# Half chunks of the output's second channel half taken from eight PSUM banks, and what is reordered with them

## The chip, the cores and the metric

The kernel runs on one core of a Trainium2 chip. The metric is the device time of one execution in microseconds (us). Three executions of the kernel before the change took 295.18, 295.45 and 297.18 us; their median is 295.45 us.

## The reference

The input is q, k and v of shape 4 x 5056 x 256 and the weights of a soft mixture of experts (8 experts with 4 slots each, 32 slots in all). Cut to what matters:

```python
qn = q / (norm(q, axis=1) + 1e-6);  kn = k / (norm(k, axis=1) + 1e-6)
a = softmax(kn.transpose(0, 2, 1) @ qn / tau)          # 256 x 256 per batch
x = (v @ a).reshape(20224, 256)
logits = x @ phi                                       # 20224 x 32
slot_input = softmax_over_rows(logits).T @ x           # 32 x 256
slot_out[e] = relu(slot_input[e] @ w1[e]) @ w2[e]      # 4 slots per expert
c = softmax_over_slots(logits)                         # 20224 x 32
return c @ slot_out                                    # 20224 x 256, 20.7 MB
```

The last line is the part that the change touches: a product of 20224 x 32 by 32 x 256, whose result has to leave PSUM through two engines and the core through the DMA queues.

## The kernel before, in words

For some 210 us the core reads q, k and v, scores, normalizes, and reduces everything to the 32 slot inputs. Then comes the expert MLP (`up`, `flip_h`, `down`) and at last the output. The order on TensorE (PE), VectorE (DVE), ScalarE (ACT) and on SyncE's DMA queue (SP) is the order in which the code is written, so each engine takes its instructions as they stand and waits where an operand is not there.

The slot outputs (32 x 256) are made in two channel halves of 128. `down(0, ...)` makes the first half in PSUM tile `O`; `fetch(0)` copies it out on DVE (tile `ob`), and `spread(0)` multiplies it by a folding matrix (matmul `fo`, L902) and copies the result on ACT to `so_a` and `so`. With that the output's first half can start while `down(1, ...)` still makes the second half. The 16 steps of `down(1, ...)` are handed out by `more(MORE[u])` between the output pieces; each step is four matmuls in the code, eight in the trace, where each f32 product shows as two instructions. When all 16 are out, `fetch(1)` and `spread(1)` bring the second half to `so`.

The output rows come as 20 chunks of up to 1024 rows, in ten pairs (`PAIRS`). A pair has a tile `cT` of combine weights, turned by four transposes on PE (`flip_c`, tile `cTp`) and copied by ACT.

- The first four pairs (`HALVED = 4`) go out as half chunks of 512 KB: `half_chunk(i, z, h)` is pair i, chunk z, channel half h. The text calls the eight of the first channel half u0 to u7 and the eight of the second u8 to u15, in the order of the code. A half chunk is eight small matmuls into four PSUM tiles `oph` (L923; sixteen in the trace), four copies from PSUM to SBUF (`oh<-oph`, L926: tiles 0 and 2 by ACT, 1 and 3 by DVE) and one DMA (L927). The `oph` tiles come from pool `pq` with five banks.
- The other six pairs go out as whole chunks of 1 MB or 0.98 MB, o1 to o12 in the text: eight matmuls `op` of 256 columns (L991), four copies of 512 columns (L998), and DMAs (L1003), out of pool `po` with eight banks, which opens when the half chunks are done.

Ahead of each half chunk of the second channel half and of each whole chunk stands a product with the identity (L919, 256 columns; L988, 512 columns) into the first of its tiles, which the real matmuls then overwrite. The result doesn't depend on it.

Between the pieces DVE and ACT work on the softmax over slots of the later chunks: `combine_some(n)` takes the next n steps of a list (`top` L798, `less` L801, `total` L807 to L809, `share` L812 on DVE; `powers` L804 on ACT). `HALFC` and `POPS` say how many.

Of the kernel before, what the change touches and what calls it, by code (L numbers as in the profile page):

```python
# [8 lines left out]
F32 = mybir.dt.float32  # L9
# [8 lines left out]
def colnorm_attention_soft_moe(  # L18
# [11 lines left out]
    nc = tc.nc  # L30
    B, N, C = q.shape
    E, _, F = w1.shape
    P = 128
    J = 8
    S = 32
    G = 4
# [6 lines left out]
    HALVED = 4  # L43
    MLPC = (1, 2, 2, 2, 3, 2, 1, 1)
    FINAL = 1
    MORE = (0, 2, 2, 3, 3, 3, 3, 0)
    HALFC = (0, 1, 1, 1, 1, 0, 1, 0)
    POPS = (1, 0, 1, 0, 1, 0, 1, 0, 1, 1, 1, 1, 1, 1, 1, 1)
    LAG = 14
# [37 lines left out]
    ident = const.tile([P, P], F32, name="ident")  # L87
# [35 lines left out]
    def pieces(rows, ch, j0, j1):  # L123
        t0 = chunks[ch][0]
        jm = min(j1, JL) if ch == NCH - 1 else j1
        lo = t0 + P * j0
        yield slice(0, P), slice(j0, jm), rows[lo : lo + P * (jm - j0), :].rearrange("(p j) c -> p j c", j=jm - j0)
        if jm < j1:
            lo = t0 + P * JL
            yield slice(0, TL), slice(JL, J), rows[lo : lo + TL, :].rearrange("(p j) c -> p j c", j=1)  # L130
# [204 lines left out]
    def combine_some(n):  # L335
        while steps and (n or steps[0][0].__name__ == "powers"):
            f, h = steps.pop(0)
            f(h)
            stepped.append(f)
            n -= f.__name__ != "powers"  # L340
# [400 lines left out]
    def big(t, name):  # L741
        if t == "v":
            return vpool.tile([P, J, C], F32, tag="v", name=name)
        return wpool.tile([P, J, C], F32, tag=t, name=name, bufs=5)
# [18 lines left out]
    for step in TAIL.split():  # L763
# [13 lines left out]
        x = big("t", f"vt{pb_}_{ch}").rearrange("p (m x) c -> p m (x c)", m=2)  # L777
        n = min(P * J, N - chunks[ch][0])
# [83 lines left out]
    CH = C // 2  # L862
# [3 lines left out]
    def down(h, r, fs):  # L866
        for f in fs:
            for g in range(G):
                nc.tensor.matmul(  # L869
                    O[h][S * g : S * g + S, :],  # L870
                    hTs[r][:, f, S * g : S * g + S],
                    w2t[G * r + g][:, h, f * CH : f * CH + CH],
                    start=r == 0 and f == 0,
                    stop=r == 1 and f == NF - 1,
                )

    cTs = {}

    def flip_c(i, pool=None):
        tp = (pool or ps_t).tile([P, 4, P], F32, tag="op" if pool else "T", name=f"cTp{i}")  # L880
        for x in range(4):
            b, ch = divmod(PAIRS[i][x // 2], NCH)
            assert len(stepped) >= ready_at(b, ch), (i, len(stepped))
            t = ch * J + HJ * (x % 2)
            nc.tensor.transpose(tp[:, x, :], nat[b][:, t : t + HJ, :].rearrange("p j s -> p (j s)"), ident)  # L885
        cTs[i] = bpool.tile([P, J, P], F32, tag="vD", name=f"cT{i}", bufs=4)
        if pool:
            return tp
        nc.scalar.copy(cTs[i][:, :4], tp)

    so_a = bpool.tile([P, CH], F32, tag="aT", name="so_a")
    so = bpool.tile([P, C], F32, tag="ssb", name="so")
    obs, fos = [], []

    def fetch(h):
        ob = bpool.tile([P, C], F32, tag="gs" if h else "dg", name=f"ob{h}")[:, :CH]
        nc.vector.tensor_copy(ob, O[h])
        obs.append(ob)

    def spread(h):  # L900
        fo = ps_t.tile([P, 4, P], F32, tag="T", name=f"fo{h}")[:, 0]
        nc.tensor.matmul(fo, fold4, obs[h], start=True, stop=True)  # L902
        if h == 0:
            nc.scalar.copy(so_a, fo)
        nc.scalar.copy(so[:, CH * h : CH * h + CH], fo)

    halves = {}

    def half_chunk(i, z, h):
        if z == 0:  # L910
            halves[i, h] = vpool.tile([P, 2, J, CH], F32, tag="v", name=f"oh{i}_{h}")
        ot = halves[i, h][:, z]
        rhs = so[:, CH:] if h else so_a
        b, ch = divmod(PAIRS[i][0], NCH)
        r0 = b * N + chunks[ch][0] + P * J * h + P * HJ * z
        dst = out[r0 : r0 + P * HJ, :].rearrange("(p a) c -> p (a c)", p=P)
        ops = [pq.tile([P, 2, CH], F32, tag="op", name=f"oph{i}_{h}_{z}_{t}") for t in range(G)]
        if h:
            nc.tensor.matmul(ops[0].rearrange("p x c -> p (x c)"), ident, so, start=True, stop=True)  # L919
        for x in range(2):  # L920
            for t in range(G):
                rows = slice(S * t, S * t + S)
                nc.tensor.matmul(ops[t][:, x, :], cTs[i][rows, 2 * z + x, :], rhs[rows, :], start=True, stop=True)  # L923
        for t in range(G):
            copy = nc.vector.tensor_copy if t % 2 else nc.scalar.copy
            copy(ot[:, t::G, :], ops[t])  # L926
        nc.sync.dma_start(dst, ot.rearrange("p j c -> p (j c)"))  # L927
        if z and h:
            cTs.pop(i)
# [10 lines left out]
    pq = ps_h.enter_context(tc.tile_pool(name="pq", bufs=5, space=PSUM, reuse_waits="tile"))  # L940
# [12 lines left out]
    def more(n):  # L953
        for _ in range(n):
            r, f = second.pop(0)
            down(1, r, (f,))

    for u in range(2 * HALVED):
        more(MORE[u])
        if second == [] and len(obs) == 1:  # L960
            fetch(1)
        half_chunk(u // 2, u % 2, 0)
        if u in (2, 4):
            flip_c(u // 2 + 1)
        if u == 2 * HALVED - 2:
            spread(1)
        combine_some(HALFC[u])
    pops = iter(POPS)
    for i in range(HALVED):
        for z in range(2):  # L970
            half_chunk(i, z, 1)
            combine_some(next(pops, 0))
        if i == 1:
            flip_c(HALVED)
    ps_h.close()
    ps_m.close()
    ps_x.close()
    po = ctx.enter_context(tc.tile_pool(name="po", bufs=8, space=PSUM, reuse_waits="tile"))
    for i, pair in enumerate(PAIRS):
        if i < HALVED:  # L980
            continue
        cT = cTs.pop(i)
        for z, y in enumerate(pair):
            b, ch = divmod(y, NCH)
            ot = vpool.tile([P, J, C], F32, tag="v", name=f"o{b}_{ch}")
            ops = [po.tile([P, 2, C], F32, tag="op", name=f"op{b}_{ch}_{t}") for t in range(G)]
            held = cT[:, :4].rearrange("p x c -> p (x c)")
            nc.tensor.matmul(ops[0].rearrange("p x c -> p (x c)"), ident, held, start=True, stop=True)  # L988
            for x, t in [(x, t) for x in range(2) for t in range(G)]:
                rows = slice(S * t, S * t + S)  # L990
                nc.tensor.matmul(ops[t][:, x, :], cT[rows, 2 * z + x, :], so[rows, :], start=True, stop=True)  # L991
            n = min(next(pops, 0), len(steps))
            flip = z == 0 and i + 1 < len(PAIRS)
            if flip:
                tp = flip_c(i + 1, po)
            for t in range(G):
                copy = nc.scalar.copy if t % 2 == 0 or t == 1 and n and z else nc.vector.tensor_copy
                copy(ot[:, t::G, :], ops[t])  # L998
            if flip:
                nc.scalar.copy(cTs[i + 1][:, :4], tp)  # L1000
            combine_some(n)
            for ps, js, dst in pieces(out[b * N : b * N + N, :], ch, 0, J):
                nc.sync.dma_start(dst, ot[ps, js, :])  # L1003
# [52 lines left out]
```

## Time and profile before

| | |
|---|---|
| median of three executions | 295.45 us |
| the profiled execution's own time | 295.44 us |
| its span in the trace | 293.3 us |
| PE busy | 273.4 us, 93% |
| DVE busy | 226.9 us, 77% |
| ACT busy | 196.2 us, 67% |
| DMA | 113.03 MB, mean 385 GB/s |
| first output DMA issued | 234.06 us |
| last output DMAs issued | from 284.75 us |
| last matmul started, last DVE copy started | 282.9 us, 284.0 us |

The span runs from the first to the last instruction on the core; 2.14 us of the execution's time lie outside it. The 16 DMA engines are shared by all transfers, and "DMA share" is their mean busy share: 1.00 is full, and a window of two or three microseconds can show a little more. All times in the trace are counted from the span's start.

### The profile page before, as it was taken

The numbers are of one execution on the slowest core, as the hardware profiler recorded it, in microseconds if no ns is written. First come the engines' busy times: TensorE is split into PE (matmuls) and PEld (weight loads), VectorE is DVE, ScalarE is ACT, GpSimd is POOL, SyncE is SP. The second block draws the span as 40 slices with busy tenths as digits, with TensorE's granted clock in tenths as the row PEclk, the third lists the DMA queues.
The fourth block names the chain that finished last, engine by engine and source line by source line (L and its number), as shares of the span: only waits on it lengthen the run. The fifth ranks groups of instructions, "written<-read, shape, count | busy, mean of one in ns | idle before, by whom it ended". The sixth has DMA issues, their size and how long they took to land.

```text
span 293.3 us, 6456 instructions
## 1 busy us (share of the span) xinstructions
PE 273.4 (93%) x2552; PEld 211.7 (72%) x2552; DVE 226.9 (77%) x338; ACT 196.2 (67%) x321; POOL 8.4 (3%) x22
## 2 busy tenths in 40 slices
PE   7998999999999999999999999789999999999960
PEld 4787999788898788788878878466654776655520
DVE  1379997998898998989898992669777598768550
ACT  2698676797779799876989923545616474577540
POOL 0000001000010010001001001000000000000000
PEclk9999999999999999999999999999999999999995
DMA  6999999999999999899979999999999998979996
GB/s 218 417 416 405 398 404 421 415 426 370 408 404 422 422 370 381 345 407 358 393 306 327 401 419 401 421 425 405 421 417 416 394 362 328 374 312 404 400 423 257
DMA packets 27228, 113.03 MB, mean 385 GB/s; under 512 B 3264, under 2 KB 4288, under 8 KB 23104
## 3 DMA queue, kind: packets, MB, share of 16 engines
q1 hardware_dynamic: 27200, 112.64, 96.6%
q8 instruction: 20, 0.33, 0.4%
q14 instruction: 8, 0.07, 0.1%
HBM read 91.92 MB, written 20.71 MB: 384 GB/s over the span
## 4 chain that ended last, share of the span: by engine, by line
PE 58%; DVE 9%; ACT 6%; issue 4%; DVEq 0%; ACTq 0%
PE S L240 21%; PE L L388 4%; PE op L991 4%; PE G L516 4%; PE oph L923 4%; PE op L988 4%; PE O L869 3%; PE H L842 2%; DVE hl L203 2%; PE cTp L885 2%; PE oph L919 2%; PE vTp L361 2%; DVE all L219 2%; ACT et L464 1%; PE Mp L318 1%
## 5 line engine op out<-in xcount | busy, mean ns | idle before, releaser
L240 PE MATMUL S<-raw 128*128 128x256 f32 x364 | 84.9, 385 | 0.6 <-DMA raw<-in_k_dram 0.6
L209 ACT ACTIVATE sq<-raw 128x2048 f32<-128x2048 f32 x40 | 76.1, 1909 | 8.3 <-DMA raw<-in_k_dram 5.9
L240 PEld LDWEIGHTS S<-raw 128*128 128x128 f32 x364 | 68.0, 192 | 14.5 <-issue 5.9
L219 DVE TENSOR_TENSOR all<-all,sq 128x2048 f32<-128x2048 f32 x32 | 73.1, 2284 | 6.6 <-ACT sq L209 6.0
L240 PE MATMUL S<-hl 128*128 128x256 f32 x414 | 57.2, 290 | 2.8 <-DVE hl L203 2.6
L240 PEld LDWEIGHTS S<-hl 128*128 128x128 f32 x414 | 51.7, 191 | 5.6 <-DVE hl L203 4.0
L198 ACT CAST hl<-raw 128x1024 fp32r<-128x1024 f32 (+2 forms) x37 | 36.5, 987 | 15.6 <-PE S L240 14.6
L203 DVE TENSOR_TENSOR hl<-raw,hl 128x1024 fp32r<-128x1024 f32 (+2 forms) x37 | 42.5, 1147 | 5.4 <-ACT hl L198 5.4
L998 ACT COPY o<-op 128x512 f32<-128x512 f32 x27 | 14.4, 591 | 10.1 <-issue 4.8
L998 DVE COPY o<-op 128x512 f32<-128x512 f32 x21 | 13.7, 687 | 9.1 <-PE op L991 6.0
L516 PE MATMUL G<-v,dn 128*32 128x256 f32 x320 | 19.5, 381 | 1.3 <-ACT lt L404 1.1
L926 ACT COPY oh<-oph 128x256 f32<-128x256 f32 x32 | 10.3, 375 | 9.7 <-PE oph L923 8.6
L926 DVE COPY oh<-oph 128x256 f32<-128x256 f32 x32 | 12.0, 417 | 6.1 <-PE oph L923 6.0
L361 PE MATMUL vTp<-ident,v 128*128 128x128 f32 x120 | 16.1, 276 | 0.6 <-DVE ssb L291 0.6
L217 DVE TENSOR_TENSOR all<-sq,sq 128x2048 f32<-128x2048 f32 x4 | 9.1, 2268 | 9.7 <-ACT sq L209 9.7
L516 PEld LDWEIGHTS G<-v,dn 128*32 128x32 f32 x320 | 11.4, 110 | 6.2 <-ACT gs L532 1.7
L361 PEld LDWEIGHTS vTp<-ident,v 128*128 128x128 f32 x120 | 13.9, 146 | 2.2 <-DVE ssb L291 0.8
L991 PEld LDWEIGHTS op<-so,cT 32*128 32x128 f32 x192 | 8.7, 184 | 9.4 <-issue 9.1
L991 PE MATMUL op<-so,cT 32*128 32x256 f32 x192 | 13.8, 400 | 0.0
L373 ACT COPY vT<-vTp 128x512 f32<-128x512 f32 x22 | 11.8, 587 | 1.9 <-PE vTp L361 1.9
L988 PE MATMUL op<-cT,ident 128*128 128x512 f32 x24 | 13.0, 623 | 0.0
L388 PE MATMUL L<-vD,M 128*32 128x256 f32 (+1 forms) x144 | 11.5, 379 | 0.0
(130 smaller groups left out, 305.5 us busy)
## 6 DMA issues: line engine op xcount, KB each, us to landing
raw<-in_q_dram SPq DMA_DIRECT2D x35, 512.0 KB, 7.4
raw<-in_k_dram SPq DMA_DIRECT2D x35, 512.0 KB, 8.2
v<-in_v_dram SPq DMA_DIRECT2D x16, 1024.0 KB, 10.7
w<-in_moe_w_dram SPq DMA_DIRECT2D x8, 1024.0 KB, 13.8
w<-in_moe_w_dram SPq DMA_DIRECT2D x16, 512.0 KB, 10.0
out_dram<-oh SPq DMA_DIRECT2D x16, 512.0 KB, 3.7
out_dram<-o SPq DMA_DIRECT2D x8, 1024.0 KB, 6.2
vD<-in_v_rows_dram SPq DMA_DIRECT2D x15, 512.0 KB, 8.7
```

Source lines behind the costliest of these rows:

```text
L198: nc.scalar.copy(hl[u][:, 0, :, :ns], raw_of(u)[:, :, :ns])
L203: nc.vector.tensor_tensor(hl[u][:, 1, :, :ns], raw_of(u)[:, :, :ns], hl[u][:, 0, :, :ns].bitcast(F32), op=ALU.subtract)
L209: nc.scalar.activation(sq[u], raw_of(u), AF.Square)
L219: nc.vector.tensor_tensor(st[b]["all"], st[b]["all"], sq.pop(u), op=ALU.add)
L240: nc.tensor.matmul(sps[:, m, :], lhs, rhs, start=r == 0 and part == 0 and x == 0 and y == 0 and m == 0, stop=r == H - 1 and part == 1 and ...
L361: nc.tensor.transpose(tp[:, jj, :], vt[:, 4 * hh + jj, P * m : P * m + P], ident)
L388: nc.tensor.matmul(L[S * g : S * g + S, :je, :], M[:, m, :], st[b]["vT", ch, m][:, :je, S * g : S * g + S], start=m == 0, stop=m == 1,)
L516: nc.tensor.matmul(gp[S * g : S * g + S, :], tiles[c][:, j, :], vt[:, j, :], start=c == 0 and j < G, stop=c == n - 1 and j >= G,)
L926: copy(ot[:, t::G, :], ops[t])
L988: nc.tensor.matmul(ops[0].rearrange("p x c -> p (x c)"), ident, held, start=True, stop=True)
L991: nc.tensor.matmul(ops[t][:, x, :], cT[rows, 2 * z + x, :], so[rows, :], start=True, stop=True)
L998: copy(ot[:, t::G, :], ops[t])
```

## The change

It touches only what happens after 232 us.

- Pool `po` with its eight banks opens before the half chunks of the second channel half, and these take their tiles from it. For that, everything that uses the older pools has to be over: `fetch(1)` and `spread(1)` come right after u7, where `spread(1)` stood after u6. The transposes for the fifth pair (`flip_c(HALVED)`) also write a tile of `po`.
- `MORE` hands out the 16 steps of `down(1, ...)` in four visits of four (before u1, u3, u5, u7) instead of six visits of two or three (before u1 to u6).
- The turned combine weights of the third and fourth pair come after u1 and u3 instead of after u2 and u4.
- The identity product ahead of the half chunks stands only before every second one, as one of 256 and one of 128 columns; ahead of whole chunks it has 384 columns instead of 512.
- In u8, u10, u12 and u14, where DVE has a softmax step to do, ACT takes three of the four copies instead of two.

```diff
-    MORE = (0, 2, 2, 3, 3, 3, 3, 0)
+    MORE = (0, 4, 0, 4, 0, 4, 0, 4)
...
-    def half_chunk(i, z, h):
+    def half_chunk(i, z, h, n=0):
...
-        ops = [pq.tile([P, 2, CH], F32, tag="op", name=f"oph{i}_{h}_{z}_{t}") for t in range(G)]
-        if h:
-            nc.tensor.matmul(ops[0].rearrange("p x c -> p (x c)"), ident, so, start=True, stop=True)
+        ops = [banks[0].tile([P, 2, CH], F32, tag="op", name=f"oph{i}_{h}_{z}_{t}") for t in range(G)]
+        if h and not z:
+            for x in range(2):
+                nc.tensor.matmul(ops[x].rearrange("p x c -> p (x c)")[:, : C - x * CH], ident, so[:, : C - x * CH], start=True, stop=True)
...
-            copy = nc.vector.tensor_copy if t % 2 else nc.scalar.copy
+            copy = nc.scalar.copy if t % 2 == 0 or t == 1 and n else nc.vector.tensor_copy
...
+    banks = [pq]
     for u in range(2 * HALVED):
         more(MORE[u])
         if second == [] and len(obs) == 1:
             fetch(1)
         half_chunk(u // 2, u % 2, 0)
-        if u in (2, 4):
-            flip_c(u // 2 + 1)
-        if u == 2 * HALVED - 2:
-            spread(1)
+        if u in (1, 3):
+            flip_c(u // 2 + 2)
         combine_some(HALFC[u])
-    pops = iter(POPS)
-    for i in range(HALVED):
-        for z in range(2):
-            half_chunk(i, z, 1)
-            combine_some(next(pops, 0))
-        if i == 1:
-            flip_c(HALVED)
+    spread(1)
     ps_h.close()
     ps_m.close()
     ps_x.close()
     po = ctx.enter_context(tc.tile_pool(name="po", bufs=8, space=PSUM, reuse_waits="tile"))
+    banks[0] = po
+    pops = iter(POPS)
+    for i in range(HALVED):
+        for z in range(2):
+            n = next(pops, 0)
+            half_chunk(i, z, 1, n)
+            combine_some(n)
+        if i == 1:
+            tp = flip_c(HALVED, po)
+            nc.scalar.copy(cTs[HALVED][:, :4], tp)
...
-            nc.tensor.matmul(ops[0].rearrange("p x c -> p (x c)"), ident, held, start=True, stop=True)
+            nc.tensor.matmul(
+                ops[0].rearrange("p x c -> p (x c)")[:, : 3 * P], ident, held[:, : 3 * P], start=True, stop=True
+            )
```

Three places show how the order moves. In the names, `oph_0_1_3` is the PSUM tile of channel half 0, chunk 1 of its pair, tile 3, and the number behind it tells one tile from the next.

On PE between u5 and u6, before the change, steps of the second half of `O` stand between the two half chunks:

```order
L923 MATMUL oph_0_1_2_2629<-so_a,cT_2540 128x128
L923 MATMUL oph_0_1_3_2630<-so_a,cT_2540 128x128
L869 MATMUL O<-w_4_1845,hT_2384 32x128
L869 MATMUL O<-w_5_1847,hT_2384 32x128
L869 MATMUL O<-w_6_1849,hT_2384 32x128
```

At the same place of the change u6 follows u5 at once:

```order
L924 MATMUL oph_0_1_2_2625<-so_a,cT_2521 128x128
L924 MATMUL oph_0_1_3_2626<-so_a,cT_2521 128x128
L924 MATMUL oph_0_0_0_2641<-so_a,cT_2582 128x128
L924 MATMUL oph_0_0_1_2642<-so_a,cT_2582 128x128
L924 MATMUL oph_0_0_2_2643<-so_a,cT_2582 128x128
L924 MATMUL oph_0_0_3_2644<-so_a,cT_2582 128x128
```

So nothing on PE lies between the two any more, while the five banks of `pq` stay as they were.

On PE at the end of the first channel half, before: the spreading product `fo` stands between u6 and u7, and u7's eight matmuls come between it and the first use of `so` (the row with `ident`).

```order
L923 MATMUL oph_0_0_3_2662<-so_a,cT_2609 128x128
L902 MATMUL fo_2676<-ob_2656,fold_98 128x128
L923 MATMUL oph_0_1_0_2680<-so_a,cT_2609 128x128
L923 MATMUL oph_0_1_1_2681<-so_a,cT_2609 128x128
L923 MATMUL oph_0_1_2_2682<-so_a,cT_2609 128x128
L923 MATMUL oph_0_1_3_2683<-so_a,cT_2609 128x128
L923 MATMUL oph_0_1_0_2680<-so_a,cT_2609 128x128
L923 MATMUL oph_0_1_1_2681<-so_a,cT_2609 128x128
L923 MATMUL oph_0_1_2_2682<-so_a,cT_2609 128x128
L923 MATMUL oph_0_1_3_2683<-so_a,cT_2609 128x128
L919 MATMUL oph_1_0_0_2698<-so,ident 128x256
L923 MATMUL oph_1_0_0_2698<-so,cT_2452 128x128
```

The same place of the change, from u7's last two matmuls on:

```order
L924 MATMUL oph_0_1_2_2679<-so_a,cT_2582 128x128
L924 MATMUL oph_0_1_3_2680<-so_a,cT_2582 128x128
L902 MATMUL fo_2694<-ob_2675,fold_98 128x128
L920 MATMUL oph_1_0_0_2704<-so,ident 128x256
L920 MATMUL oph_1_0_1_2705<-so,ident 128x128
L924 MATMUL oph_1_0_0_2704<-so,cT_2452 128x128
```

`fo` moved behind u7, and the next matmul reads `so`, which ACT makes from `fo`'s result.

On DVE at the same place, before: the copy `ob` (L897) stands ahead of u6's copies (`oph_0_0`), and each half chunk has two copies.

```order
L897 COPY ob_2656<-O 128x128
L926 COPY oh_0_2658<-oph_0_0_1_2660 128x2x128
L926 COPY oh_0_2658<-oph_0_0_3_2662 128x2x128
L812 TENSOR_TENSOR nat_107<-nat_107,cm_0_1865 128x640
L926 COPY oh_0_2658<-oph_0_1_1_2681 128x2x128
L926 COPY oh_0_2658<-oph_0_1_3_2683 128x2x128
L926 COPY oh_1_2697<-oph_1_0_1_2699 128x2x128
L926 COPY oh_1_2697<-oph_1_0_3_2701 128x2x128
L807 TENSOR_REDUCE cm_1_1866<-nat_107 128x20
```

With the change:

```order
L927 COPY oh_0_2640<-oph_0_0_1_2642 128x2x128
L927 COPY oh_0_2640<-oph_0_0_3_2644 128x2x128
L812 TENSOR_TENSOR nat_107<-nat_107,cm_0_1865 128x640
L897 COPY ob_2675<-O 128x128
L927 COPY oh_0_2640<-oph_0_1_1_2678 128x2x128
L927 COPY oh_0_2640<-oph_0_1_3_2680 128x2x128
L927 COPY oh_1_2703<-oph_1_0_3_2707 128x2x128
L807 TENSOR_REDUCE cm_1_1866<-nat_107 128x20
```

`ob` moved behind u6's copies and the softmax step L812, and u8 (`oph_1_0`) has one copy on DVE where it had two.

## The prediction

> **What bounds the kernel now.** I read the page's slices first, then a table by windows over the output stage, then the DMA queue's own timeline and the chain of waits.
>
> ```profile
> PE 273.4 (93%) x2552; PEld 211.7 (72%) x2552; DVE 226.9 (77%) x338; ACT 196.2 (67%) x321; POOL 8.4 (3%) x22
> PE   7998999999999999999999999789999999999960
> DMA  6999999999999999899979999999999998979996
> ```
>
> PE looks like the bound, but in the last slice DMA is still busy when PE shows 0. The windows (busy us of PE, PEld, DVE, ACT, POOL, then granted clock, DMA share, GB/s) say more:
>
> ```profile
> 233.00:245.00 12.00, 12.00 (x264) 9.07 (x260) 10.21 (x24) 7.87 (x22) 0.00 (x0) 1.00 0.85 337
> 245.00:248.00 3.00, 3.00 (x44) 1.98 (x40) 2.38 (x8) 1.29 (x4) 0.00 (x0) 1.00 0.98 392
> 248.00:258.00 10.00, 10.00 (x126) 6.51 (x127) 6.78 (x17) 4.50 (x14) 0.00 (x0) 1.00 0.91 359
> 258.00:261.00 3.00, 3.00 (x24) 1.51 (x22) 2.35 (x4) 2.67 (x6) 0.00 (x0) 1.00 0.58 232
> 261.00:264.00 3.00, 3.00 (x28) 1.51 (x26) 2.38 (x5) 2.43 (x6) 0.00 (x0) 1.00 0.93 361
> 264.00:290.00 26.00, 19.28 (x172) 9.97 (x172) 14.16 (x24) 12.89 (x25) 0.00 (x0) 0.93 1.01 411
> ```
>
> From 264 us on DMA is full to its end, with PE idle for the last of it. So the kernel ends when a fixed number of output bytes has been moved, and **what counts is DMA's idle time between the first output and 264 us**: 12 x 0.15 = 1.80 us, then 3 x 0.02 = 0.06, 10 x 0.09 = 0.90, 3 x 0.42 = 1.26 and 3 x 0.07 = 0.21, 4.23 us in all. An edit that makes an engine faster is worth only the part of this that it fills. With all of it filled the time would be 295.44 - 4.23 = 291.2. At 411 GB/s a half chunk (524 KB) takes 1.27 us and a whole one 2.55. Once the queue is drained, the gap between two issues less 1.27 is idle time. The issues of u0, u7, u8, u9, u15, o1 and o2:
>
> ```profile
> 234.06 0.34 SPq L927 DMA_DIRECT2D out_dram<-oh  x1
> 245.09 0.33 SPq L927 DMA_DIRECT2D out_dram<-oh  x1
> 246.41 0.33 SPq L927 DMA_DIRECT2D out_dram<-oh  x1
> 248.26 0.33 SPq L927 DMA_DIRECT2D out_dram<-oh  x1
> 256.59 0.33 SPq L927 DMA_DIRECT2D out_dram<-oh  x1
> 259.28 0.33 SPq L1003 DMA_DIRECT2D out_dram<-o  x1
> 262.04 0.34 SPq L1003 DMA_DIRECT2D out_dram<-o  x1
> ```
>
> u15 to o1 is 2.69 us, the largest hole; u8 to u9 is 1.85; u8 to u15 takes 10.18 us for seven half chunks, where DMA needs 8.9.
>
> **The first channel half: four visits of O.** What each piece costs on PE is in the chain of waits (start, us, line, count):
>
> ```profile
> 225.88 0.87 PE O L869 x32
> 232.53 0.66 PE oph L923 x16
> 233.19 0.57 PE O L869 x16
> 235.85 0.59 PE cTp L885 x4
> 236.43 0.79 PE O L869 x24
> 242.82 0.42 PE fo L902 x2
> 245.53 0.63 PE oph L919 x2
> 255.74 1.05 PE op L988 x2
> 256.79 1.08 PE op L991 x16
> 258.46 0.86 PE op L988 x2
> ```
>
> Sixteen instructions of O take 0.57, twenty-four 0.79: eight more cost 0.22, so a visit has about 0.13 us of its own and one of 32 takes 1.01 (0.87 in the row at 225.88 is the other bound). Six visits become four: 2 x 0.13 = 0.26 us of PE saved. But DVE is nearly as full here:
>
> ```profile
> 234.48 0.76 DVE L926 COPY oh<-oph 128x256 f32<-128x256 f32 x2 [0.48 <-PE oph L923]
> 235.16 0.82 DVE L801 TENSOR_TENSOR nat<-nat,cm 128x640 f32<-128x640 f32 x1
> 235.90 0.76 DVE L926 COPY oh<-oph 128x256 f32<-128x256 f32 x2
> 240.06 0.81 DVE L807 TENSOR_REDUCE cm<-nat 128x20 f32<-128x640 f32 x1
> 241.43 0.76 DVE L926 COPY oh<-oph 128x256 f32<-128x256 f32 x2
> 242.23 0.29 DVE L897 COPY ob<-O 128x128 f32<-128x128 f32 x1
> ```
>
> By the starts of these rows two copies hold DVE 0.68 us, 0.34 each (the last one ends 0.42 after its start), a step holds it 0.74, the three-part step 1.37. The walk, with copies starting 0.06 after the last matmul (before: chain 245.53, issue 246.41, which is 0.06 + 0.76 + 0.06): u0's matmuls end at 233.19 as before. O 1.01 and oph 0.66 put u1's end at 234.86, cTp and u2 at 236.11, u3 at 237.78, u4 at 239.03, u5 at 240.70. On DVE u1's copies start at 234.92, u2's at 236.34, u3's wait for PE until 237.84, u4's start at 239.26, and u5's, behind the three-part step, at 239.26 + 0.68 + 1.37 = 241.31. There is now nothing on PE between u5 and u6, and with five banks u6's third tile needs the bank that DVE's first copy of u5 empties, about 241.73; six of its eight matmuls remain (0.50), so u6 ends at 242.25 and its copies start at 242.31. O's last visit ends at 243.26. `ob` now stands behind u6's copies and L812, at 242.31 + 0.68 + 0.74 = 243.73, and ends at 244.02. u7's matmuls end at 243.92, its DVE copies start at 244.05, its issue is at **244.87, against 245.09**: 0.22 us less idle time in this stretch, 1.58 left of 1.80.
>
> **The hand-over to the second channel half.** Before, u7's matmuls covered `fo` and the copy to `so`. Now they are in line, and three ACT instructions count:
>
> ```profile
> 243.37 0.29 ACT L905 COPY so<-fo 128x128 f32<-128x128 f32 x1
> 244.07 0.65 ACT L926 COPY oh<-oph 128x256 f32<-128x256 f32 x2 [0.42 <-PE oph L923]
> L926 ACT COPY oh<-oph 128x256 f32<-128x256 f32 x32 | 10.3, 375 | 9.7 <-PE oph L923 8.6
> ```
>
> `fo` runs from 244.07 to 244.49. On ACT u7's copies (243.98 to 244.63) stand ahead of the copy to `so`, which ends at 244.92. Queued behind it on PE is the identity product and all the rest of the output. 256 columns cost 0.63, 512 cost 1.05, so 384 columns cost 0.84; that 256 + 128 in two pieces cost as one of 384 is my assumption (1.05 if the second pays the fixed 0.21 again). From 244.97 on, 0.84 + 0.66 give u8's end at 246.47, against 245.53. Then ACT has three copies where it had two, 0.65 + 0.27 = 0.92, and u8's issue comes at **247.5, against 246.41**. The gap u7 to u8 is 2.63 us; less 1.27 that is 1.36 us idle, where there was 0.06. Bounds: 0.4 if the identity product finds room in the wait for `so` (less 0.84) and ACT's queue costs nothing (less 0.1); 1.9 if its second piece pays the 0.21 and the line through DVE is another 0.3 late. I keep 1.36, since each piece has its row.
>
> **Eight banks and the rest of the half chunks.** Per pair PE now needs 0.66 + 0.66 + 0.84 = 2.16 us; DVE one copy, a step and two copies, 0.34 + 0.74 + 0.76 = 1.84 (2.47 with the three-part step); ACT five copies, about 1.5. DMA needs 2.55. Before, PE alone needed 2 x (0.63 + 0.66) = 2.58 and waited for banks besides. So **DMA is the slowest from here on**, but for u9: DVE copies one tile of u8 at 246.53, then takes the three-part step, then u9's two copies at 248.24; issue 249.06, 1.56 after u8, 0.29 idle. After that no gap: PE ends u9 at 247.13, u10 at 248.63, u11 at 249.45 (it waits for u9's last bank, 249.01), cTp at 250.04, then 1.50 and 0.66 in turn: u15 at 254.36, o1 at 254.36 + 0.84 + 1.08 = 256.28. DVE's two copies of 512 columns then set o1's issue:
>
> ```profile
> 257.93 1.29 DVE L998 COPY o<-op 128x512 f32<-128x512 f32 x2 [1.40 <-PE op L991]
> ```
>
> 256.35 + 1.29 + 0.06 = **257.70, against 259.28**. Counted from u9's issue, seven half chunks keep DMA busy to 249.06 + 8.9 = 257.95, so o1 is 0.25 early: the hole closes with little to spare. Its 0.98 MB last 2.38 us, to 260.33; with the same 2.76 us to o2 as before, o2 is issued at 260.46, 0.13 late. From o3 on PE has 4.65 - 2 x 0.21 = 4.23 us of work for a pair of whole chunks (1.05 + 0.86 + 2 x 1.08 + 0.59, with 384 columns instead of 512), DMA 5.1. Twelve products shortened by 0.21 are 2.5 us of PE that lie beside a full DMA and are worth nothing at the end.
>
> **Sum.** Idle after: 1.58 + 1.36 + 0.29 + 0.13 = 3.36 us, against 4.23: 0.87 gained. Counting gaps overstates idle time a little: before, u8 to u9 (1.85 - 1.27), u15 to o1 (2.69 - 1.27) and o1 to o2 (2.76 - 2.38) alone give 2.38 of the 2.43 that the windows from 245 to 264 show, in which the short gaps between u9 and u15 lie too. So the gaps counted for the change are if anything too large, and I take 1.1 rather than 0.87. Made against the profiled execution's 295.44 (span 293.3 and 2.14 outside, which stay), which is the median of 295.45 for this purpose: **294.3 us**.
>
> **Rivals.** *The hand-over is cheap* (16 in 100): if `so` is ready as u7's copies end and PE catches up, the 1.3 us come back, and if the first stretch shrinks too, up to 2.9 us are gained: 291.7 to 293.2, say 292.6. For it: DVE, which makes `ob` late, was idle 0.48 us in the row at 234.48. Against: three instructions on three engines in line, each with a row. *The change brings nothing* (17 in 100): o1 is only 0.25 early and o2 already late, so half a microsecond more on DVE or ACT there, or a hand-over of 2 us, brings the idle time back to 4.2: 295.4. *The clock falls* (7 in 100), the case that is slower. When PE stops, the granted clock goes to 0.50:
>
> ```profile
> 286.00:287.00 1.00, 0.00 (x0) 0.00 (x0) 0.00 (x0) 0.00 (x0) 0.00 (x0) 0.75 1.00 418
> 287.00:288.00 1.00, 0.00 (x0) 0.00 (x0) 0.00 (x0) 0.00 (x0) 0.00 (x0) 0.50 0.99 415
> 195.00:198.40 3.40, 2.31 (x35) 1.62 (x30) 2.48 (x8) 2.60 (x10) 0.00 (x0) 1.00 1.01 424
> ```
>
> After the change PE waits for banks in each pair of half chunks, 2.16 us of work in 2.55 and less identity product to fill the rest. If the clock swung between 1.00 and 0.50, 0.75 in the mean, a pair of whole chunks would take PE 4.23 / 0.75 = 5.64 us, 0.54 over DMA's 5.1, six times 3.2 us; and a pair of half chunks 2.88, 0.33 over, four times 1.3; less the gain, 295.44 + 4.5 - 1.1 = 298.8. It decides below a mean clock of 4.23 / 5.1 = 0.83. Against it: from 195 to 198.4 PE is busy 68% of the time and the clock stays 1.00; 85% is foreseen here. The Trainium skill, "TensorE: Matmul & The Clock Gate", section "A second HAM failure mode: psum-queue depth-cycling", speaks for it: there, cycling through PSUM banks made PE idle in small pieces often enough that the clock swung between half and full. By that rule the time would be near 298.8; the window at 195 us, which holds idle pieces too, bears it out so little that I give it no more than its 7.
>
> **Chances and range.** Forecast, 293.2 to 295.1: 60 in 100. With the two neighbours the range is 292.4 to 295.8; it leaves out the far end of the cheap hand-over and the clock. A measurement of this kernel tells about 1% (under 292.5 or over 298.4) from no change: faster 0.13 (most of the cheap hand-over's case), same 0.80, slower 0.07 (the clock).
>
> **What would show it.** Right: u7's DMA near 244.9 and u8's near 247.5 with DMA nearly idle between; o1 near 257.7; DMA share 1.0 from about 249 on; last matmul near 279, some 8 us ahead of DMA's end. Wrong: a granted clock under 1.00 before PE ends; an idle DMA between u15 and o2; or u8 before 246.5, which would mean that the line through `ob`, `fo` and `so` is shorter than its rows.

## The result, and the profile after

The changed kernel takes **293.83 us** (median of twelve executions, 292.81 to 295.32) against 295.61 us for the kernel before in the same comparison (twelve, 294.63 to 297.18). The ratio is 0.9939, 95% interval 0.9916 to 0.9961: 1.8 us, with an interval of 1.2 to 2.5. The profiled execution took 294.12 us with a span of 292.1. The forecast was 294.3, its range 292.4 to 295.8.

The windows of the changed kernel, cut as before (busy us of PE, PEld, DVE, ACT, POOL, then granted clock, DMA share, GB/s):

```profile
233.00:245.00 12.00, 11.31 (x255) 9.06 (x252) 10.01 (x24) 7.71 (x21) 0.00 (x0) 1.00 0.90 356
245.00:248.00 3.00, 3.00 (x48) 2.47 (x52) 1.36 (x4) 1.48 (x5) 0.00 (x0) 1.00 0.57 228
248.00:258.00 10.00, 10.00 (x144) 7.62 (x144) 8.00 (x18) 6.91 (x20) 0.00 (x0) 1.00 0.98 385
258.00:261.00 3.00, 3.00 (x34) 1.76 (x28) 2.15 (x4) 2.53 (x6) 0.00 (x0) 1.00 1.03 404
261.00:264.00 3.00, 3.00 (x30) 1.55 (x32) 2.93 (x7) 2.89 (x7) 0.00 (x0) 1.00 0.99 365
264.00:288.50 24.50, 15.20 (x150) 8.51 (x142) 11.77 (x20) 10.85 (x21) 0.00 (x0) 0.88 1.01 415
```

The idle time of DMA moved rather than went: 248 to 261, where 2.16 us had been lost, is full now, and 245 to 248, which had been full, lost 3 x 0.43 = 1.29 us. In all it is 1.20 + 1.29 + 0.20 + 0.03 = 2.72 us, against 4.23. That the first of these terms fell from 1.80 to 1.20 is not the change's doing. The last weight loads (`w`, issued from 225.25 on, 10.0 us from issue to landing) still move when u0 is issued and fill that window by a different amount in each run: a second profile of the same changed kernel (last line) has a share of 0.85 there, 1.80 us, as before.

```profile
w<-in_moe_w_dram SPq DMA_DIRECT2D x2, 512.0 KB, 10.0
233.00:245.00 12.00, 11.31 (x242) 9.01 (x234) 9.61 (x24) 7.27 (x20) 0.00 (x0) 1.00 0.85 336
```

The issues of u0, u7, u8, u9, u15, o1 and o2 in the changed kernel:

```profile
233.91 0.34 SPq L928 DMA_DIRECT2D out_dram<-oh  x1
244.84 0.33 SPq L928 DMA_DIRECT2D out_dram<-oh  x1
247.39 0.33 SPq L928 DMA_DIRECT2D out_dram<-oh  x1
248.91 0.33 SPq L928 DMA_DIRECT2D out_dram<-oh  x1
255.56 0.33 SPq L928 DMA_DIRECT2D out_dram<-oh  x1
257.56 0.93 SPq L1009 DMA_DIRECT2D out_dram<-o  x2
260.10 0.34 SPq L1009 DMA_DIRECT2D out_dram<-o  x1
```

The hole is between u7 and u8, and the timeline of the changed kernel shows the line that makes it (start, us, engine; in brackets idle time and what ended it):

```profile
243.58 0.28 DVE L897 COPY ob<-O 128x128 f32<-128x128 f32 x1
243.91 0.49 PE L902 MATMUL fo<-ob,fold 128*128 128x128 f32 x2
243.98 0.65 ACT L927 COPY oh<-oph 128x256 f32<-128x256 f32 x2 [1.20 <-PE oph L924]
244.51 0.28 ACT L905 COPY so<-fo 128x128 f32<-128x128 f32 x1
244.85 0.92 PE L920 MATMUL oph<-so,ident 128*128 128x256 f32 x4 [0.45 <-ACT so L905]
```

### The profile page after: what moved, and what is told of

Its sections match the earlier page's. It is cut to its first block, busy times and chain, and to the rows that moved or that the text cites. A ratio compares the mean times of both kernels' runs of the same rounds, so it can differ in the third digit from the quotient of the medians.

```text
span 292.1 us, 6455 instructions
## 1 busy us (share of the span) xinstructions
PE 268.6 (92%) x2552; PEld 211.9 (73%) x2552; DVE 224.9 (77%) x334; ACT 197.2 (68%) x325; POOL 8.4 (3%) x22
## 4 chain that ended last, share of the span: by engine, by line
PE 57%; DVE 7%; ACT 6%; issue 3%; DMA 2%; SPq 0%; DVEq 0%; ACTq 0%
PE S L240 22%; PE op L997 4%; PE L L388 4%; PE G L516 4%; PE oph L924 4%; PE op L992 3%; PE O L869 3%; PE H L842 2%; PE cTp L885 2%; DMA raw<-in_k_dram 2%; DVE hl L203 2%; PE vTp L361 2%; ACT et L464 1%; PE oph L920 1%; PE Mp L318 1%
## 5 line engine op out<-in xcount | busy, mean ns | idle before, releaser
L927 ACT COPY oh<-oph 128x256 f32<-128x256 f32 x36 | 11.2, 383 | 7.6 <-PE oph L924 6.8
L927 DVE COPY oh<-oph 128x256 f32<-128x256 f32 x28 | 10.5, 413 | 7.0 <-PE oph L924 7.0
L992 PE MATMUL op<-cT,ident 128*128 128x384 f32 x24 | 10.4, 517 | 0.0
```

Source lines behind the costliest of these rows:

```text
L992: nc.tensor.matmul(ops[0].rearrange("p x c -> p (x c)")[:, : 3 * P], ident, held[:, : 3 * P], start=True, stop=True)
```

## The experiments

**A measure that repeats.** All kernels here are alike until the first output DMA, but that DMA's issue (u0) moves: 233.11 to 235.79 us over the profiles. The time from u0's issue to the end of the span, called the **output stage** from here on, repeats: 58.15 and 58.19 us in two profiles of the change whose u0 lay 0.49 us apart, 57.86 and 57.84 in two of the kernel with even copies. The table gives it for every run, with the gap from u7 to u8 and the time from u0 to o1, each a difference of issue times. The **end share** is the DMA share in the 5 us that end 1.5 us before the span does; behind them no output data move. Ratios are to the kernel before on the same chip.

| kernel | u0 | span | output stage | u7 to u8 | u0 to o1 | end share | median | ratio, 95% interval |
|---|---|---|---|---|---|---|---|---|
| before | 234.06 | 293.3 | 59.28 | 1.32 | 25.22 | 0.76 | 295.61 | 1 |
| the change | 233.91 | 292.1 | 58.15 | 2.55 | 23.65 | 0.71 | 293.83 | 0.9939 (0.9916 to 0.9961) |
| the change again | 233.42 | 291.6 | 58.19 | 2.55 | 23.65 | 0.70 | 293.68 | 0.9932 (0.9907 to 0.9957) |
| wide identity | 234.03 | 291.9 | 57.84 | 2.55 | 23.87 | 0.76 | 294.07 | 0.9965 (0.9939 to 0.9991) |
| early spread | 233.57 | 290.7 | 57.14 | 2.11 | 23.18 | 0.83 | 292.92 | 0.9930 (0.9902 to 0.9958) |
| even copies | 234.66 | 292.5 | 57.86 | 2.47 | 24.14 | 0.82 | 294.87 | 0.9978 (0.9957 to 0.9999) |
| even copies again | 235.49 | 293.3 | 57.84 | 2.47 | 24.15 | 0.81 | 294.01 | 0.9947 (0.9928 to 0.9967) |
| no identity | 235.79 | 292.9 | 57.15 | 1.70 | 21.04 | 0.76 | 293.41 | 0.9926 (0.9900 to 0.9952) |
| early, bare | 233.88 | 290.9 | 57.00 | 1.51 | 20.80 | 0.71 | 292.90 | 0.9899 (0.9865 to 0.9933) |
| early, bare, even | 233.11 | 290.1 | 56.96 | 1.55 | 21.62 | 0.84 | 294.21 | 0.9940 (0.9918 to 0.9963) |
| five banks | 234.13 | 295.7 | 61.57 | 2.56 | 27.60 | 0.78 | 297.28 | 1.0066 (1.0034 to 1.0097) |
| six visits | 233.76 | 291.0 | 57.27 | 2.10 | 23.30 | 0.83 | 294.06 | 0.9952 (0.9920 to 0.9985) |
| early, step later | 235.28 | 292.8 | 57.55 | 2.10 | 23.01 | 0.71 | 293.95 | 0.9940 (0.9909 to 0.9970) |
| long hand-over | 234.17 | 293.7 | 59.56 | 3.86 | 24.96 | 0.72 | 295.57 | 0.9997 (0.9974 to 1.0020) |

The 16 DMA engines do not all finish together. Idle time at the end counts like any other, and each hundredth of the end share is 0.05 us of it: 1.45 us in the change (5 x 0.29), 0.85 with the early spread. No expectation had this term. Two stages can be compared only together with their end shares, and this is done below. What sets the end share was not found.

The theory (A in the expectations): only idle time of DMA during the output counts; eight banks fill the holes from u8 on, and the hand-over to the second channel half opens a new one. The rivals: PE's work is what counts (B), the identity products hold the clock (C), the hole only moves (D), the sharing of copies is the gain (E), the banks do nothing (F), the four visits are the gain (G).

### The eight banks

```diff
-    banks[0] = po        # and po opened before the half chunks
+    # half chunks of the second half stay in pq; po opens after them, flip_c(HALVED) uses ps_t
```

> The change, but the half chunks of the second channel half keep the five banks of pool pq, and pool po opens after them as before; visits of O, late spread, identity products and sharing of copies are the change's. Theory A: a half chunk again waits for the copies of the one before it, some 1.4 us for each against DMA's 1.27, and o1 comes 2.3 to 2.7 us after u15; with the hand-over's hole still there the time is 295.3 to 296.2 us, no faster than before. Rival F (the banks do nothing, the gain is in shorter identity products and shared copies): 293.8.

297.28 us, 0.66% slower than before; the output stage is 3.4 us longer than the change's, more than expected (296.2 at most). F falls. u8 and u15 of this run, and its window:

```profile
247.62 0.33 SPq L928 DMA_DIRECT2D out_dram<-oh  x1
259.10 0.33 SPq L928 DMA_DIRECT2D out_dram<-oh  x1
248.00:258.00 10.00, 9.24 (x120) 7.79 (x113) 6.01 (x14) 5.30 (x16) 0.00 (x0) 1.00 0.79 315
```

Seven half chunks take 11.48 us, 1.64 each where I had put 1.4, because PE, DVE and ACT take turns: PE waits for ACT's copy of u8 ahead of u9's matmuls, and ACT then waits for these.

```profile
247.09 1.26 PE L924 MATMUL oph<-so,cT 32*128 32x128 f32 x14 [0.24 <-ACT oh L927]
248.18 0.65 ACT L927 COPY oh<-oph 128x256 f32<-128x256 f32 x2 [0.59 <-PE oph L924]
```

The stage is also 2.3 us longer than that of the kernel before, with the same five banks: the gap u7 to u8 is 1.24 us longer, and u8 to u15 1.30. So 3.4 us is what the banks are worth within this change; without them the rest of it costs 2.3. The banks alone, put into the kernel before, were not run.

### The hand-over, longer and shorter

Longer: u8's identity product three times.

```diff
-            for x in range(2):
+            for x in (0, 1, 0, 1, 0, 1) if i == 0 else (0, 1):
                 nc.tensor.matmul(ops[x]..., ident, so..., start=True, stop=True)
```

> The change with u8's identity product made three times (two more of 0.84 us each) and nothing else. Theory A: PE's extra 1.7 us stand where DMA has run dry, so that the gap u7 to u8 grows from 2.55 to about 4.2 us and the time by 1.3 to 1.7 us, to 295.2 to 295.6; the run with 2.5 us more of PE work beside a full DMA cost nothing. Rival B (PE's work is what counts): both should have cost the same per microsecond.

295.57 us. The two further products cost 0.65 us each, not 0.84 (2.23 us for twelve instructions against 0.92 for four), so the gap grew by 1.31 us, and the output stage by 1.41: about one to one, with the end share nearly the same.

```profile
245.12 2.23 PE L920 MATMUL oph<-so,ident 128*128 128x256 f32 x12 [0.45 <-ACT so L905]
```

Shorter: O finished a half chunk earlier, `fo` between u6 and u7.

```diff
-    MORE = (0, 4, 0, 4, 0, 4, 0, 4)
+    MORE = (0, 4, 0, 4, 0, 4, 4, 0)
...
+        if u == 2 * HALVED - 2:
+            spread(1)
         combine_some(HALFC[u])
-    spread(1)
```

> The change, but O's second half is finished one half chunk earlier (visits of four before u1, u3, u5, u6) and the product fo stands between u6 and u7, so that u7's matmuls cover the copy to so. Theory A: u8's DMA is issued near 246.0 instead of 247.39, the hole of 1.3 us in DMA between u7 and u8 shrinks to about 0.1, and the time falls by 1.0 to 1.3 us, to 292.5 to 292.8. Rival B (the work on PE is the same): no change against 293.8. Rival D (the hole only moves, because u6 comes later behind O's fourth visit): less than 0.4 us gained.

292.92 us, output stage 57.14, 1.01 us less than the change. That is the time that A gave, in part by luck: the gap fell only to 2.11 us, by 0.44, and the rest is the end share, 0.83 in place of 0.71, which is 0.60 us less idle time at the end. The direction speaks for A; the gap's 0.44 alone would have been close to D's 0.4. A new wait took part of the room that A counted on: u8's second identity product gets a bank of `po` that u7's last DVE copy has to empty first.

```profile
244.47 0.30 PEld L920 LDWEIGHTS oph<-so,ident 128*128 128x128 f32 x2 [0.62 <-DVE oh L927]
```

I tried to take that wait away by moving the DVE step L812 behind u7's copies:

```diff
-    HALFC = (0, 1, 1, 1, 1, 0, 1, 0)
+    HALFC = (0, 1, 1, 1, 1, 0, 0, 1)   # with the early spread
```

> As the run with the early spread, with the softmax step L812 moved behind u7's copies on DVE, identity products kept. Theory A: the second identity product of u8 no longer waits for u7's DVE copy; the gap u7 to u8 falls from 2.11 to 1.5 to 1.7 us, the time to 292.4 to 292.7. Rival D: u9 comes later by the moved step and nothing is gained, 292.9.

A miss: the gap stayed at 2.10, since u7's own issue came earlier by as much as its copy. The stage is 57.55, 0.60 us less than the change's, and the end share is the change's 0.71. So this run shows the early spread by itself: the gap is 0.45 us shorter and u0 to u7 0.18, 0.63 in all. And with the order of before in the first channel half:

```diff
-    MORE = (0, 4, 0, 4, 0, 4, 0, 4)
+    MORE = (0, 2, 2, 3, 3, 3, 3, 0)    # flip_c after u2 and u4, spread(1) after u6
```

> The change with the old order of the first channel half: O's second half in six visits, turned weights after u2 and u4, fo between u6 and u7; only eight banks, identity products and sharing of copies are the change's. Theory A: u7 is issued near 245.1, and the gap to u8 is about 1.9 us where the change has 2.55, so that the time is 0.2 to 0.6 below the change's, 293.2 to 293.6: the four visits and the late spread together cost, and do not bring, time. Rival G (the four visits are worth their 0.26 us and more): 294.0 or over.

The gap is 2.10, not 1.9, and the stage 57.27, 0.88 us less than the change (0.60 of it at the end) and within 0.13 of the early spread with its four visits, whose end share is the same. The median, 294.06, lies where G had put it; its interval reaches from 0.9920 to 0.9985. I go by the stage, and by it G falls: u0 to u7 takes 11.03 us here and 10.91 with the early spread, so that the four visits are worth 0.1 us, and the late spread costs 0.45 in the gap.

### The identity products

```diff
-                ops[0]...[:, : 3 * P], ident, held[:, : 3 * P], start=True, stop=True
+                ops[0]..., ident, held, start=True, stop=True      # 512 columns again
```

> The change, but with the identity product ahead of whole chunks back at 512 columns. Theory A (only idle time of DMA during the output counts): PE gets 12 x 0.21 = 2.5 us more work, all of it beside a full DMA; the time stays that of the change, 293.8 us, within 0.3. DMA stays full from 249 us on. Rival B (PE's work is what counts): the 2.5 us come back, 296.3 us, no faster than before.

294.07 us, and a stage of 57.84: 2.5 us of PE's work more, and no longer; of the 0.31 us by which it is shorter, 0.25 lie in the end share. B falls, together with the long hand-over, where 1.31 us of the same kind of work cost 1.41.

```diff
-        if h and not z:        # half chunks
-            for x in range(2): nc.tensor.matmul(ops[x]..., ident, ...)
-            nc.tensor.matmul(ops[0]..., ident, held...)      # whole chunks
```

> The change without any identity product ahead of half chunks and whole chunks. Theory A: u8's matmuls end 0.84 us earlier, so the hole between u7 and u8 shrinks by up to 0.84, and the rest lies beside a full DMA: 293.0 to 293.4 us, if the granted clock stays at 1.00. Rival C (the identity products keep the clock up): PE is busy for some 60% of 245 to 280, the clock falls to 0.50 in that stretch, PE becomes the bound, and the time is over 297.

The gap fell by 0.85 us, as one identity product costs, and the stage by 1.00, 0.25 of it at the end. PE is less busy, and the granted clock stays at 1.00 (the last matmul starts at 272.52):

```profile
248.00:258.00 10.00, 9.60 (x152) 7.98 (x152) 9.51 (x22) 8.82 (x26) 0.00 (x0) 1.00 0.96 378
264.00:272.50 8.50, 7.82 (x107) 6.10 (x104) 7.72 (x14) 7.25 (x16) 0.00 (x0) 1.00 1.01 412
```

C falls for these kernels. It had supposed PE busy for some 60%, and PE shows 96% and 92%, so what the clock would do at 60% over such a length is not shown. The two best edits together, and L812 behind u7:

```diff
# the early spread, HALFC = (0, 1, 1, 1, 1, 0, 0, 1), and no identity product in the output
```

> As the run with the early spread, and besides the softmax step L812 moved from before u7's copies on DVE to behind them, and no identity products in the output at all. Theory A: u8 no longer waits for u7's last DVE copy nor for an identity product; its DMA is issued 1.3 to 1.5 us after u7's (2.55 in the change, 2.11 with the early spread), the hole is gone, and the time is 292.0 to 292.6 us. Rival D (DMA idles elsewhere in its place): no faster than the early spread, 292.9. Rival C (the identity products keep the clock up) has fallen, since the run without them kept 1.00 until PE was done; it would give over 295 here.

292.90 us, ratio 0.9899 (0.9865 to 0.9933), the best of all: faster than before by 1.0%, and than the change by its stage, 57.00 against 58.15. The gap is 1.51. But the median is 0.3 us over the forecast and exactly what D gave, and the stage is only 0.14 us better than with the early spread alone: the gap is 0.60 us shorter, and the end share is back at 0.71, 0.60 us more idle time. In that sense D holds in part. And u8 does still wait for u7's last DVE copy, now with its first matmuls:

```profile
244.63 2.19 PE L924 MATMUL oph<-so,cT 32*128 32x128 f32 x45 [0.68 <-DVE oh L927]
```

### The sharing of copies

```diff
-            copy = nc.scalar.copy if t % 2 == 0 or t == 1 and n else nc.vector.tensor_copy
+            copy = nc.scalar.copy if t % 2 == 0 else nc.vector.tensor_copy
```

> The change, but each half chunk of the second channel half has two copies on ACT and two on DVE again. Theory A: DVE needs 2.26 us for a pair with a one-part step (2.9 with the three-part one), DMA 2.55, so that u9's DMA comes 0.3 later and o1's 0.5 to 1.2 later; with 0.25 us of cover the time rises by 0.4 to 1.2 us, to 294.2 to 295.0. Rival E (the sharing of copies is what the change gains by): all of it is gone, 295.6.

294.87 us, which reads like the expected loss; but the stage is 57.86, shorter than the change's, although o1 comes 0.49 us later after u0. So the same kernel ran once more:

> The change with even copies once more. Its first profile showed an output stage (u0's issue to the end of the span) of 57.84 us, no longer than the change's 58.19, but its median was 1.0 us over the change's. If sharing the copies is worth time (theory A as first put), the stage is over 58.3 here; if not, it is again near 57.8, and a median near 294.9 would then come from before u0's issue, one near 293.8 from the spread between runs.

The stage is 57.84, the median 294.01, u0 at 235.49: the 1.0 us was spread between runs, not DVE. It goes with the granted clock: of the first run's twelve executions the six with a mean clock of 0.981 took 295.12 to 295.79 us, the six with 0.983 to 0.988 took 293.19 to 294.62. A drop like that of the last section takes 4 x 0.35 = 1.4 of 293 us, or 0.005, off that mean.

That the stage is not longer does not mean that the copies cost DMA nothing. From u9's issue to o1's, first of the change, then of the first run with even copies:

```profile
248.91:257.56 8.65, 8.65 (x118) 6.44 (x118) 6.65 (x15) 6.02 (x18) 0.00 (x0) 1.00 0.99 391
249.91:258.80 8.89, 8.89 (x118) 6.64 (x118) 7.55 (x18) 5.07 (x14) 0.00 (x0) 1.00 0.95 376
```

DMA idles 0.44 us there where it idled 0.09, as theory A had it; the end share, 0.82 against 0.71, gives 0.55 us back. And with the early spread and no identity products:

```diff
# early, bare, with the even copies of the last diff
```

> As the early spread without identity products, with two copies on ACT and two on DVE in every half chunk of the second channel half. Theory A: with the hole at the hand-over gone DMA has work in store, so that DVE's 2.26 us for a pair stay under DMA's 2.55; u9 comes 0.3 us later behind the three-part step, and the time rises by 0 to 0.4 us, 292.9 to 293.3. Rival E (the sharing of copies is what the change gains by): 294.5 or over.

The stage is 56.96, as with shared copies (57.00); the median, 294.21, lies 1.3 us above that run's, and by it E would nearly hold. I go by the stage, which two pairs of kernels agree on: the change's gain is not the sharing of copies. Here too DMA idles more between u9 and o1 (a share of 0.91 against 0.97, 0.46 us) and less at the end (0.84 against 0.71, 0.65 us). In neither pair does sharing gain time; whether the end follows from the copies isn't shown. Part of the high median goes with the clock again: five of the twelve executions show a mean of 0.964 to 0.968 and took 294.29 to 294.94 us, and none of the nine with shared copies is under 0.969. The rest wasn't settled.

> The change itself, for comparison on the same chip as the other two and for a second profile. All theories: 293.8 us within 0.5; the gap u7 to u8 again 2.55 us. If the start of the output (u0's issue) moves by more than 0.5 us against the first profile, the spread between runs comes from before 232 us, where all kernels are alike.

293.68 us and again a gap of 2.55, with u0 0.49 us earlier, just under the half microsecond that I had set.

## Why the prediction was right

- **What bounds.** Right. Work beside a full DMA was free (wide identity), work in its hole cost 1.08 us for each (long hand-over). What it left out is the end. It took DMA as full from 264 us to its end, but in the last 5 us of data the kernel before has a share of 0.76, 1.20 us idle, and the change 0.71, 1.45. This term moves by up to 0.65 us between kernels.
- **The first channel half.** u7 was foreseen at 244.87 and came at 244.84, but u0 had moved by 0.15, so that from u0 to u7 only 0.10 us was saved (11.03 to 10.93), not 0.22; the near hit is luck. A visit of 32 takes what I had extrapolated, as the changed kernel's chain of waits shows:

```profile
233.03 1.01 PE O L869 x32
```

- **The hand-over.** u8 foreseen at 247.5, measured 247.39; the hole 1.36 foreseen, 1.29 in the window. The identity product in two pieces took 0.85 us (244.85 to 245.70), as one of 384 columns would.
- **Eight banks.** u9 249.06 foreseen, 248.91 measured; u15 255.65 and 255.56; o1 257.70 and 257.56; o2 260.46 and 260.10. Without them the stage is 3.4 us longer, so within the change this one edit carries the gain, and pays for the hand-over.
- **The sum.** The terms gave 0.87 us gained, and an estimate of what counting gaps overstates made it 1.1; the output stage gained 1.13. That this is so close is partly luck. The first stretch gave 0.10 for 0.22, and the end, which stood at nothing, cost 0.25. Against that, the idle time behind the hand-over came to 0.23 for 0.42 and the hand-over's to 1.29 for 1.36. Of the medians' 1.8 us the other 0.65 lies outside this stage, and no run explains it.
- **What was wrong.** I held o1's cover of 0.25 us to be thin, and half a microsecond more on DVE to cost the gain. Even copies made o1 0.49 us later and cost DMA some 0.35 us ahead of it, not the whole 0.87, and the stage did not grow, because the end was better. The last matmul started at 278.83, near the foreseen 279, but DMA's end lay almost 12 us behind it and not 8; the prediction's own sum would have given that.
- **The clock.** It was 1.00 to the last matmul. The Trainium skill, "TensorE: Matmul & The Clock Gate", section "A second HAM failure mode: psum-queue depth-cycling", names the swing that I took as the slower rival. The trace of this stage shows no such swing, but the change did not test it: PE shows busy all the time from u8 to its last matmul, where I had foreseen 85%. The run "early, bare, even" cycles through the eight banks with PE idle in pieces, and its clock is at 1.00 too:

```profile
258.00:261.00 3.00, 2.14 (x26) 1.26 (x28) 2.93 (x7) 3.00 (x8) 0.00 (x0) 1.00 1.02 373
```

## What to carry to other kernels

Where the last stage ends with a queue that never runs dry, add up its idle time, the uneven end included, and ask of each edit which hole it fills: within this change eight banks in place of five filled 3.4 us, and 2.5 us of matmuls removed filled nothing. An edit that needs all users of a pool to be done moves a barrier, and what was covered by the work behind it becomes a line: look for the chain that crosses the new barrier. When the effect is smaller than the spread between runs, time the stage itself from its own first event, and ask whether the time came from the hole that the edit was meant to fill.

## What the runs showed that was not expected

**The clock fell in the expert MLP**, not in the output, in two profiles. The 48 instructions of `up` in the timeline of the changed kernel, and then in that of the run without identity products:

```profile
217.42 5.36 PE L842 MATMUL H<-w,slT 128*32 128x512 f32 x48
```

```profile
217.80 6.86 PE L842 MATMUL H<-w,slT 128*32 128x512 f32 x48
```

In the second run with even copies a window at that place has the clock at 0.65, with PE shown busy throughout:

```profile
218.00:222.00 4.00, 4.00 (x28) 0.97 (x24) 3.86 (x8) 0.69 (x1) 0.00 (x0) 0.65 1.04 417
```

These two have the latest u0, 235.79 and 235.49. All kernels have the same code there, so the drop is part of the spread between runs. From the first `up` to u0 these two take 18.0 and 18.2 us, all other profiles 16.5; the rest of u0's spread lies ahead of `up`, as with the 235.28 of one profile, which has no drop.

**The stage got shorter with more work.** Wide identity and even copies gave 57.84 to 57.86 us against 58.15 and 58.19, because DMA's last transfers end more unevenly in the change. The last 5 us of data in the kernel before, the change, the first run with even copies, the early spread, and the early spread with the step later:

```profile
286.84:291.84 5.00, 0.00 (x0) 0.00 (x0) 0.00 (x0) 0.00 (x0) 0.00 (x0) 0.50 0.76 308
285.56:290.56 5.00, 0.00 (x0) 0.00 (x0) 0.00 (x0) 0.00 (x0) 0.00 (x0) 0.50 0.71 287
286.02:291.02 5.00, 0.00 (x0) 0.00 (x0) 0.00 (x0) 0.00 (x0) 0.00 (x0) 0.50 0.82 332
284.21:289.21 5.00, 0.00 (x0) 0.00 (x0) 0.00 (x0) 0.00 (x0) 0.00 (x0) 0.50 0.83 337
286.33:291.33 5.00, 0.00 (x0) 0.00 (x0) 0.00 (x0) 0.00 (x0) 0.00 (x0) 0.50 0.71 287
```

No engine works in any of them, so this is DMA's own end. The last two kernels differ by the place of one DVE step some 40 us earlier. What makes the transfers end so was not tried.
